# Last batch: weights loaded pairs ahead of their splits, two operands kept raw, last-row transposes first in the queue; v prepared one pair later

## The chip, the cores and the metric

The kernel runs on one core of one Trainium2 chip. The metric is the device time in microseconds; of several runs the median is taken. Smaller is better. The engines are PE (TensorE: matmuls, and PEld for its weight loads), ACT (ScalarE), DVE (VectorE), POOL (GpSimd) and SP (SyncE, which issues nearly all DMAs of this kernel into one queue).

## The reference

Attention without a softmax, gated by `u`, and then a mixture of experts with one expert per token and a capacity.

```python
# u, v: [8, 2496, 256], z: [8, 2496, 64], all float32
scores = (1.0 / S) * np.matmul(z, z.transpose(0, 2, 1))
attn = np.maximum(scores, 0.0) ** 2
x = (u * np.matmul(attn, v)).reshape(B * S, D)          # 19968 x 256

logits = x @ w_gate                                     # 8 experts
expert_idx = np.argmax(logits, axis=1)
gate_w = softmax(logits)[arange(N), expert_idx]
for e in range(8):
    tok_idx = tokens of expert e, the 80 with the largest gate_w
    h = np.maximum(x[tok_idx] @ w1[e], 0.0)             # w1[e]: 256 x 1024
    out[tok_idx] = gate_w[tok_idx, None] * (h @ w2[e])  # w2[e]: 1024 x 256
```

All other rows of the output are zero.

## The kernel before

**Numbers.** A float32 operand of a matmul is split into a high and a low part (`ah` and `al`, two halves of `vt`, `w1h` and `w1l` and so on), and each product takes three matmuls. The high part is a cast on ACT (or DVE), the low part a subtraction on DVE.

**Attention.** Each batch has 20 tiles of 128 tokens. The loop runs over `steps`, which are (batch `b`, chunk `qc` of 512 query tokens, pair `r` of key tiles): 5 chunks of 10 pairs in each of 8 batches. The last chunk has 448 tokens. The scores are symmetric, so a block below the diagonal is not computed a second time: `mirror` transposes it in squares on DVE into a tile `x` and writes that to memory (`y`), and `mirror_back` reads it into a tile `blk` by four DMAs before `mirrored` uses it. A step does this, in this order: the scores of the pair two steps ahead (`scores`: two matmuls a tile into one of three PSUM tiles `s`, the relu on ACT at L316, the square, the cast `ah`, the subtraction `al`, or only the cast at L296 and the subtraction for a mirrored block), the products of its own pair with `v` (`attend`), the bookkeeping of the chunk before (`finished`: the pieces of `x` for the gate, the DMA transposes of `xf` into `xq` by `chunk_store`, the write of `xs` by `chunk_store2`, logits, gate, counts), the loads of the next batch's `z` and `v`, zeros for the output, and in the last batch `weights_ahead`.

**Order.** PE, ACT, DVE and SP issue in the order in which the code is written (`manual_schedule`). Each engine, and the DMA queue of SP, is therefore a line: what waits at its head holds all that stands behind it.

**v of the next batch.** In a batch's last chunk, `prep_v` splits the next batch's five groups of `v`, one at each odd pair: the cast at L105 on ACT, the subtraction at L146 on DVE. Behind the split of group `g` the load of group `g + 2` is issued, since there are two raw buffers, `vraw`.

**Weights ahead.** The 16 weight operands of the 8 experts (`w1` and `w2`) are handled as halves of 512 KB. Ten halves, `order_w`, are loaded and split during the last two chunks of the last batch (`at_w`). A half goes into a raw buffer (`load_raw`; L586) and is split by `split_w` (L596 on ACT, L597 on DVE) in the very next pair. The split parts live in tiles that attention no longer needs (`places`):

```python
for p, raw in list(w_raw.items()):
    split_w(*p, w_raw.pop(p), V)
```

**The end.** After the last pair come the last chunk's `x`, its logits, the gate, the transposes and the write of `xs`, the count, and `blocks`. The expert stage (`ahead`) looks up the tokens of the first two experts, runs `WARM` idle matmuls (4 before the first, 9 before the second lookup's work) on PE, gathers the tokens by an indirect DMA of POOL (`xg<-xs`, L1035), and then runs eight experts, while `split` takes the next half of the weights that are left (their subtraction goes to DVE or POOL) and `loads` issues the load of another.

Of the kernel before, what the change touches and what calls it, by code (L numbers as in the profile page):

```python
# [8 lines left out]
F32 = mybir.dt.float32  # L9
# [10 lines left out]
P = 128  # L20
# [5 lines left out]
def attn_moe_kernel(ctx, tc, zT, uT, v, wg, w1, w2, out, seq, cap):  # L26
# [5 lines left out]
    nc = tc.nc  # L32
    V = nc.vector
    B, _, SP = zT.shape
# [8 lines left out]
    NQ = NT // QT  # L43
# [22 lines left out]
    NA = 4  # L66
# [491 lines left out]
    NPIECE = 2048  # L558
    wt = {}
    n_early = [0]  # L560
    places = []
    late = {}

    def wtile(name):
        if late.get("own"):
            pool, tag = late["own"], "w"
        else:
            i = n_early[0] % (NA + NX + NV + NW)
            n_early[0] += 1
            pool, tag = (places + [(late["pool"], "w")] * NW if "pool" in late else places)[i]  # L570
        return pool.tile([P, NPIECE], F32R, tag=tag, name=f"{name}_{nid()}")

    def load_raw(e, which, part, after=None):

        n = DC if which == 1 else FC
        if which == 1:
            src = w1[e].rearrange("(c p) f -> p c f", p=P)
        else:
            src = w2[e].rearrange("(j p) d -> p j d", p=P)
        pool, tag = (late["raw"], "wraw") if "raw" in late else (zpool, "vraw")  # L580
        raw = pool.tile([P, NPIECE // 2], F32, tag=tag, name=f"wraw_{e}_{which}_{part}")
        rv = raw.rearrange("p (c f) -> p c f", c=n // 2)
        if after:

            after.memset(raw[:, :1], 0.0)
        nc.sync.dma_start(out=rv, in_=src[:, part * n // 2:(part + 1) * n // 2])  # L586
        return rv

    def split_w(e, which, part, rv, eng):
# [19 lines left out]

    ON_V = {(0, 8), (0, 12), (0, 16)}  # L610

    order_w = [(0, 1), (0, 2), (1, 1), (1, 2), (2, 1)]
    at_w = [(NQ - 2, r) for r in (2, 4, 6, 8)] + [(NQ - 1, r) for r in range(1, 7)]
    WAT = {(B - 1,) + at: (*order_w[n // 2], n % 2) for n, at in enumerate(at_w)}
    WARM = 4, 9
    steps = [(b, qc, r) for b in range(B) for qc in range(NQ) for r in range(NP)]
    ET = mybir.EngineType
    v_raw, z_raw, w_raw = {}, {}, {}

    def weights_ahead(b, qc, r):  # L620
        for p, raw in list(w_raw.items()):
            split_w(*p, w_raw.pop(p), V)
        if (b, qc, r) in WAT:
            if not places:

                xt, vv = (sqpool, "x"), (vpool, "vt")
                nb = B * NQ * (NQ - 1) // 2
                a4 = [(apool, f"a{n % NA}") for n in range(nb - NA, nb)]
                places.extend([xt, xt, xt, vv, a4[0], vv, xt, a4[1], a4[2], vv, a4[3], vv, vv, vv])
            p = WAT[b, qc, r]  # L630
            w_raw[p] = load_raw(*p)

    def finished(b, qc, r):

# [41 lines left out]
    with tc.manual_schedule(engines={ET.PE, ET.Activation, ET.DVE, ET.SP}):  # L676
        prep_zc(0, 0, raw0)
        prep_zd(0, 0, raw0)
        prep_zc(0, 1, raw12[:, 0])
        scores(0, 0, 0)  # L680
        prep_v(0, 0, vraw0, nc.scalar, V)
        scores(0, 0, 2)
        v_raw[0, 1] = vraw1
        z_raw.update({(0, 2): raw12[:, 1], (0, 3): raw34[:, 0], (0, 4): raw34[:, 1]})
        constants()
        prev = None
        for i, (b, qc, r) in enumerate(steps):
            last = b == B - 1 and qc == NQ - 1
            now[0] = i
            if r == 0 and prev:  # L690
                chunk_x(*prev)
            if (b, qc) == (0, 0) and r in (0, 2, 4):
                prep_zc(0, r // 2 + 2, z_raw.pop((0, r // 2 + 2)))
            if i + LOOK < len(steps):
                nb, nqc, nr = steps[i + LOOK]
                scores(nb, nqc, 2 * nr)
            if b == 0 and qc == 0:
                if r % 2 == 0 and r < 8:
                    g = r // 2 + 1
# [12 lines left out]
            if r == 2:  # L712
                prep_u(b, qc)
            if b + 1 < B:
                if r == 1:
                    z_raw[b + 1, qc] = load_z(b + 1, qc)
                if r == 9:
                    prep_zc(b + 1, qc, z_raw.pop((b + 1, qc)))
                if qc == NQ - 2 and r == 8:
                    for g in range(2):  # L720
                        v_raw[b + 1, g] = load_v(b + 1, g)
                if qc == NQ - 1:
                    g = r // 2
                    if r % 2 == 1:
                        prep_v(b + 1, g, v_raw.pop((b + 1, g)), nc.scalar, V)
                        if g + 2 < NQ:
                            v_raw[b + 1, g + 2] = load_v(b + 1, g + 2)
            if nb < B and r == 1:
                prep_zd(nb, nqc)
            if r == 5:  # L730
                zero_out(b * NQ + qc, B * NQ)
            if b == B - 1 and qc >= NQ - 2:
                weights_ahead(b, qc, r)
            mirror_back()
            if r == NP - 1:
                prev = b, qc

        chunk_tiles(*prev)
        for kk, c in ((3, 0), (2, 0), (3, 1), (1, 0), (2, 1), (1, 1)):
            attend(*prev, NT - kk, [c])  # L740
            if kk == 1:
                chunk_x_last(*prev, c)
        chunk_logits_last(*prev)
        gate_top(b, NQ - 1, NQ)
        gate(b, NQ - 1, NQ)
        chunk_store(*prev)
        chunk_store2(*prev)
        kb = B * BPB
        count_last(kb - 2, kb)
        blocks(ps_m, "m", gp, oh, kb - 2, kb)  # L750
# [403 lines left out]
    def ahead(empty, block, fetch, pe_table, pe_block, pe_fetch, within, token, whole, ffn_x, ffn_xl,  # L1154
# [2 lines left out]
        ET = mybir.EngineType  # L1157

        pieces = [(e, w, part) for e in range(E) for w in (1, 2) for part in range(2)
                  if (e, w, part) not in WAT.values()]  # L1160
        ready = []

        def loads(n, after=None):
            for p in pieces[:n]:
                ready.append((p, load_raw(*p, after)))
            del pieces[:n]

        def look(i):
            if i < NU:
                block(i)  # L1170
                fetch(i)
                within(i)
# [19 lines left out]
        with tc.manual_schedule(engines={ET.PE, ET.Activation, ET.DVE, ET.Pool}):  # L1192
# [102 lines left out]
```

## Time and profile before

| | |
|---|---|
| median of 3 runs | 1478.59 us (1478.79, 1476.03, 1478.59) |
| the profiled execution | 1480.12 us, span 1478.4 us |
| mean granted TensorE clock | 0.976 |
| PE busy | 1396.2 us (94% of the span) |
| DMA queue of SP | 84.2% of 16 engines' span |
| HBM | 153.48 MB read, 126.46 MB written |

The profiled execution is one more run beside the three. In its page a digit of the second part is the busy share of a fortieth of the span (37 us) in tenths; in a timeline a row has the start, the duration, the engine, the line, the operation with its tiles, and in brackets the idle time before it with what ended it. A row of the waits has an engine and what it was to do, the releaser, the sum, the count and the longest. Names as `blk`, `wraw` and `xs` are the program's.

### The profile page before, as it was taken

The numbers are of one execution on the slowest core, as the hardware profiler recorded it, in microseconds if no ns is written. First come the engines' busy times: TensorE is split into PE (matmuls) and PEld (weight loads), VectorE is DVE, ScalarE is ACT, GpSimd is POOL, SyncE is SP. The second block draws the span as 40 slices with busy tenths as digits, with TensorE's granted clock in tenths as the row PEclk, the third lists the DMA queues.
The fourth block names the chain that finished last, engine by engine and source line by source line (L and its number), as shares of the span: only waits on it lengthen the run. The fifth ranks groups of instructions, "written<-read, shape, count | busy, mean of one in ns | idle before, by whom it ended". The sixth has DMA issues, their size and how long they took to land. (4 is left out here: it accounts for less than half of the span.)

```text
span 1478.4 us, 19494 instructions
## 1 busy us (share of the span) xinstructions
PE 1396.2 (94%) x7083; PEld 1144.3 (77%) x7083; DVE 1078.6 (73%) x1530; ACT 983.7 (67%) x1263; POOL 45.6 (3%) x50
## 2 busy tenths in 40 slices
PE   8999999999999999999999999999999999958587
PEld 6788878887888878887788877887788888846466
DVE  7776788677876788767876688767876688636585
ACT  7776667667776676667776677766776578735264
POOL 0000000000000000000000000000000000000074
PEclk9999999999999999999999999999999999979688
DMA  6799879995999979995999969995999959887363
GB/s 197 209 243 214 211 211 208 238 240 153 253 235 214 235 202 208 237 237 147 232 252 218 253 176 220 238 248 145 229 251 217 260 156 226 225 206 198 70 206 124
DMA packets 300102, 311.97 MB, mean 211 GB/s; under 512 B 136184, under 2 KB 228224, under 8 KB 289760
## 3 DMA queue, kind: packets, MB, share of 16 engines
q1 hardware_dynamic: 299040, 309.11, 84.2%
q0 software_dynamic: 960, 1.56, 0.4%
q8 instruction: 57, 0.93, 0.3%
q14 instruction: 45, 0.37, 0.1%
HBM read 153.48 MB, written 126.46 MB: 189 GB/s over the span
## 5 line engine op out<-in xcount | busy, mean ns | idle before, releaser
L345 PE MATMUL acc<-al,vt 128*128 128x512 f32 (+1 forms) x1520 | 590.6, 389 | 8.0 <-DVE al L54 7.8
L343 PE MATMUL acc<-ah,vt 128*128 128x512 f32 (+1 forms) x1520 | 590.6, 389 | 3.4 <-ACT ah L296 1.6
L344 PE MATMUL acc<-ah,vt 128*128 128x512 f32 (+1 forms) x1520 | 589.1, 388 | 1.2 <-DVE vt L146 1.2
L54 DVE TENSOR_TENSOR al<-a,ah 128x1024 fp32r<-128x1024 f32 (+1 forms) x240 | 291.2, 1213 | 146.8 <-ACT ah L105 137.3
L345 PEld LDWEIGHTS acc<-al,vt 128*128 128x128 f32 x1520 | 287.8, 189 | 67.9 <-DVE al L54 15.3
L343 PEld LDWEIGHTS acc<-ah,vt 128*128 128x128 f32 x1520 | 288.4, 190 | 60.8 <-ACT ah L296 4.6
L344 PEld LDWEIGHTS acc<-ah,vt 128*128 128x128 f32 x1520 | 288.4, 190 | 55.5 <-DVE vt L146 2.0
L316 ACT ACTIVATE a<-s 128x512 f32<-128x512 f32 (+1 forms) x480 | 257.7, 589 | 87.1 <-PE s L313 77.2
L296 ACT CAST ah<-blk 128x1024 fp32r<-128x1024 f32 x160 | 166.3, 1048 | 141.8 <-DMA blk<-y 65.9
L317 ACT ACTIVATE a<-a 128x1024 f32<-128x1024 f32 (+1 forms) x240 | 253.0, 1054 | 7.6
L54 DVE TENSOR_TENSOR al<-blk,ah 128x1024 fp32r<-128x1024 f32 x160 | 192.3, 1214 | 81.7 <-ACT ah L296 80.0
L257 DVE STREAM_TRANSPOSE x<-a 128x512 f32<-128x512 f32 x320 | 207.5, 686 | 0.0
L313 PE MATMUL s<-zd,zc 128*128 128x512 f32 (+1 forms) x480 | 187.4, 391 | 0.1
L105 ACT CAST ah<-a 128x1024 fp32r<-128x1024 f32 x139 | 146.0, 1050 | 4.4
L312 PE MATMUL s<-zc,zc 128*128 128x512 f32 x320 | 131.2, 410 | 5.1 <-ACT a L316 4.9
L107 DVE CAST ah<-a 128x1024 fp32r<-128x1024 f32 (+1 forms) x101 | 68.6, 680 | 49.9 <-ACT a L317 49.7
L313 PEld LDWEIGHTS s<-zd,zc 128*128 128x128 f32 x480 | 90.8, 189 | 15.2 <-issue 0.5
L312 PE MATMUL s<-zc 128*128 128x512 f32 (+1 forms) x160 | 64.9, 406 | 31.0 <-ACT a L316 31.0
L105 ACT CAST vt<-vraw 128x1024 fp32r<-128x1024 f32 (+3 forms) x56 | 45.0, 831 | 65.3 <-DMA vraw<-v 65.3
L146 DVE TENSOR_TENSOR vt<-vraw,vt 128x1024 fp32r<-128x1024 f32 (+1 forms) x40 | 46.7, 1167 | 45.4 <-ACT vt L105 45.2
L312 PEld LDWEIGHTS s<-zc,zc 128*128 128x128 f32 x320 | 60.1, 188 | 23.5 <-ACT a L316 13.4
L373 ACT CAST xb<-xf 128x1024 bf16<-128x1024 f32 (+1 forms) x39 | 40.0, 1027 | 56.7 <-DVE xf L362 56.7
(156 smaller groups left out, 846.6 us busy)
## 6 DMA issues: line engine op xcount, KB each, us to landing
y<-x SPq DMA_DIRECT2D x80, 1024.0 KB, 5.5
blk<-y SPq DMA_DIRECT2D x320, 256.0 KB, 8.2
out<-idle SPq DMA_DIRECT2D x40, 512.0 KB, 5.9
vraw<-v SPq DMA_DIRECT2D x32, 512.0 KB, 8.9
ut<-uT SPq DMA_DIRECT2D x32, 512.0 KB, 5.2
xs<-xq SPq DMA_DIRECT2D x32, 512.0 KB, 7.8
wraw<-w SPq DMA_DIRECT2D x32, 512.0 KB, 5.0
zd<-zc SPq DMA_DIRECT2D x78, 128.0 KB, 3.8
```

What stands on the lines that cost most here:

```text
L54: V.tensor_tensor(out=o, in0=a, in1=b, op=op)
L105: eng.copy(out=o, in_=i)
L107: eng.tensor_copy(out=o, in_=i)
L257: V.transpose(out=x[:, :, :, t].rearrange("p n k s -> p k n s"), in_=a)
L296: nc.scalar.copy(out=natural(ah), in_=src)
L312: nc.tensor.matmul(s[:, :nq], zk, zc[:, :nq], start=True, stop=False)
L313: nc.tensor.matmul(s[:, :nq], zk, zd[:, :nq], start=False, stop=True)
L316: nc.scalar.activation(out=a[:, h, :nq], in_=s[:, :nq], func=AF.Relu)
L317: nc.scalar.activation(out=a[:, :, :nq], in_=a[:, :, :nq], func=AF.Square)
L343: nc.tensor.matmul(o, vt[:, t, 0, cs], ah, start=k == 0, stop=False)
L344: nc.tensor.matmul(o, vt[:, t, 1, cs], ah, start=False, stop=False)
L345: nc.tensor.matmul(o, vt[:, t, 0, cs], al, start=False, stop=False)
```

## The change

1. In the last batch, the loads and splits of weights have two tables, `LOADS` and `SPLITS`. Eight halves (experts 0 and 1) are loaded at pairs 6 and 7 of chunk 2, 0, 2, 5 and 8 of chunk 3, and 2 and 4 of chunk 4; they are split at pairs 0, 2, 5 and 8 of chunk 3 and 2, 4, 5 and 7 of chunk 4. A half's load stands behind the split of the half two before it, in whose raw buffer it lands.
2. Both halves of expert 2's `w1` (at pair 4 of chunk 4) and of its `w2` (pair 6) are loaded into free tiles of attention and stay unsplit (`kept`). The expert stage splits them: one more `split(V, V)` ahead of the first expert's tokens, and the others where the next halves were split before. The list `places` is written anew for that, and `loads` counts the buffers that the kept ones do not use.
3. `WARM` is 4 and 12.
4. `chunk_store` of the last chunk is written ahead of its logits and gate.
5. `prep_v` stands at pairs 2, 4, 6, 8 and 9 of the last chunk.

```diff
+    early = [(e, w, part) for e in range(2) for w in (1, 2) for part in range(2)]
+    qa, qb, qz = NQ - 3, NQ - 2, NQ - 1
+    LOADS = dict(zip([(qa, 6), (qa, 7), (qb, 0), (qb, 2), (qb, 5), (qb, 8), (qz, 2), (qz, 4)], early))
+    SPLITS = dict(zip([(qb, 0), (qb, 2), (qb, 5), (qb, 8), (qz, 2), (qz, 4), (qz, 5), (qz, 7)], early))
+    RAW = {(qz, 4): (2, 1), (qz, 6): (2, 2)}
-    order_w = [(0, 1), (0, 2), (1, 1), (1, 2), (2, 1)]
-    at_w = [(NQ - 2, r) for r in (2, 4, 6, 8)] + [(NQ - 1, r) for r in range(1, 7)]
-    WARM = 4, 9
+    WARM = 4, 12
...
-    def weights_ahead(b, qc, r):
-        for p, raw in list(w_raw.items()):
-            split_w(*p, w_raw.pop(p), V)
+    def weights_ahead(qc, r):
...
+        if (qc, r) in SPLITS:
+            p = SPLITS[qc, r]
             split_w(*p, w_raw.pop(p), V)
+        if (qc, r) in LOADS:
+            p = LOADS[qc, r]
             w_raw[p] = load_raw(*p)
+        if (qc, r) in RAW:
+            e, which = RAW[qc, r]
+            pool, tag = late["kept"].pop(0)
+            raw = pool.tile([P, NPIECE], F32, tag=tag, name=f"wall_{e}_{which}")
+            for part in range(2):
+                rv, src = raw_part(raw[:, part * NPIECE // 2:(part + 1) * NPIECE // 2], e, which, part)
+                nc.sync.dma_start(out=rv, in_=src)
+                kept.append(((e, which, part), rv))
...
                 if qc == NQ - 1:
-                    g = r // 2
-                    if r % 2 == 1:
+                    g = (r - 1) // 2 if r < 9 else 4
+                    if r in (2, 4, 6, 8, 9):
                         prep_v(b + 1, g, v_raw.pop((b + 1, g)), nc.scalar, V)
...
+        chunk_store(*prev)
         chunk_logits_last(*prev)
         gate_top(b, NQ - 1, NQ)
         gate(b, NQ - 1, NQ)
-        chunk_store(*prev)
         chunk_store2(*prev)
...
-        ready = []
+        ready = list(kept)
         def loads(n, after=None):
+            n = min(n, NR - sum(1 for r in ready if r not in kept))
...
             look(3)
+            split(V, V)
             whole(0)
```

The next two pieces are the SP queue in the last batch, from the middle of chunk 2 to the middle of chunk 3, before and after. A row is a line, the DMA, and its tiles: `wraw_1_0` is the raw half 0 of a `w1`, `y_4_2` a block of scores written for chunk 4, `blk_3_2` one that is read for chunk 3; the number at the end of a name only counts.

```order
L236 DMA out<-idle 128x4x256
L261 DMA y_4_2_11909<-x_4_2_11852 128x2048
L278 DMA blk_3_2_11923<-y_3_2_11823 32x4x512 x4
L278 DMA blk_4_0_11928<-y_4_0_11263 32x4x512 x4
L278 DMA blk_4_1_11963<-y_4_1_11625 32x4x512 x4
L412 DMA_TRANSPOSE xq_2_12009<-xf_2_11968 128x8x128 x2
L120 DMA zd_4_12012<-zc_4_10974 64x512
L121 DMA zd_4_12012<-zc_4_10974 64x512
L278 DMA blk_4_2_12015<-y_4_2_11909 32x4x512 x4
L159 DMA ut_3_12037<-uT 128x2x512
L586 DMA wraw_1_0_12039<-w 128x1024
```

```order
L236 DMA out<-idle 128x4x256
L589 DMA wraw_1_0_11893<-w 128x1024
L261 DMA y_4_2_11911<-x_4_2_11852 128x2048
L589 DMA wraw_1_1_11925<-w 128x1024
L278 DMA blk_3_2_11927<-y_3_2_11823 32x4x512 x4
L278 DMA blk_4_0_11932<-y_4_0_11263 32x4x512 x4
L278 DMA blk_4_1_11967<-y_4_1_11625 32x4x512 x4
L589 DMA wraw_2_0_12000<-w 128x4x256
L412 DMA_TRANSPOSE xq_2_12019<-xf_2_11972 128x8x128 x2
L120 DMA zd_4_12022<-zc_4_10974 64x512
L121 DMA zd_4_12022<-zc_4_10974 64x512
```

The first half stood behind the blocks, the transposes and `ut`; now two halves stand ahead of `blk_3_2`, and the third ahead of the transposes.

ACT in the same place, at the start of chunk 3, before and after: `w1h` is the cast of a weight half, `ah_3_8` that of a mirrored block, `a_3_12` the relu of a computed one.

```order
L373 CAST xb_2_11969<-xf_2_11968 128x1024
L296 CAST ah_3_6_11992<-blk_3_1_11655 128x1024
L296 CAST ah_3_8_12020<-blk_3_2_11923 128x1024
L381 CAST xb_2_11969<-xr_2_11970 128x1024
L296 CAST ah_3_10_12041<-blk_3_2_11923 128x1024
L596 CAST w1h_52_12059<-wraw_1_0_12039 128x1024
L316 ACTIVATE a_3_12_12063<-s_3_12_12064 128x512
```

```order
L373 CAST xb_2_11973<-xf_2_11972 128x1024
L599 CAST w1h_52_11996<-wraw_1_0_11893 128x1024
L296 CAST ah_3_6_12002<-blk_3_1_11655 128x1024
L296 CAST ah_3_8_12030<-blk_3_2_11927 128x1024
L381 CAST xb_2_11973<-xr_2_11974 128x1024
L599 CAST w1h_52_11996<-wraw_1_1_11925 128x1024
L296 CAST ah_3_10_12053<-blk_3_2_11927 128x1024
L316 ACTIVATE a_3_12_12071<-s_3_12_12072 128x512
```

The first cast of a weight moved three places up, and the second one is now among the mirrored blocks of this chunk too.

The end of the SP queue, from the loads of the last chunk to the first expert's, before and after; `wall` is an operand that is kept raw, `xs<-gall` the write of the gate, `wtab` that of the lookup table, `xs<-xq` the last row's `x`.

```order
L586 DMA wraw_1_1_12465<-w 128x1024
L555 DMA wtab<-wb_12520 64x256
L586 DMA wraw_2_0_12654<-w 128x4x256
L586 DMA wraw_2_1_12656<-w 128x4x256
L501 DMA xs<-gall 128x4x1 x2
L412 DMA_TRANSPOSE xq_4_12580<-xf_4_12523 128x7x128 x2
L1255 TENSOR_LOAD flag
L1255 ISA x2
L421 DMA xs<-xq_4_12580 128x6x256
```

```order
L647 DMA wall_2_12460<-w 128x4x256 x2
L555 DMA wtab<-wb_12516 64x256
L589 DMA wraw_1_0_12650<-w 128x1024
L412 DMA_TRANSPOSE xq_4_12542<-xf_4_12519 128x7x128 x2
L589 DMA wraw_1_1_12652<-w 128x1024
L501 DMA xs<-gall 128x4x1 x2
L421 DMA xs<-xq_4_12542 128x6x256
```

The transposes moved ahead of the gate's write and of one half of the experts' own loads.

ACT in the last chunk of batch 6, where the groups of the next batch's `v` are cast (`vt_0` to `vt_2`), before and after:

```order
L296 CAST ah_4_6_10731<-blk_4_1_10431 128x1024
L105 CAST vt_0_10753<-vraw_0_10681 128x4x256
L296 CAST ah_4_8_10761<-blk_4_2_10485 128x1024
L381 CAST xb_3_10708<-xr_3_10709 128x1024
L296 CAST ah_4_10_10780<-blk_4_2_10485 128x1024
L105 CAST vt_1_10798<-vraw_1_10683 128x4x256
L296 CAST ah_4_12_10803<-blk_4_3_10702 128x1024
```

```order
L296 CAST ah_4_6_10731<-blk_4_1_10431 128x1024
L296 CAST ah_4_8_10756<-blk_4_2_10485 128x1024
L381 CAST xb_3_10708<-xr_3_10709 128x1024
L105 CAST vt_0_10775<-vraw_0_10681 128x4x256
L296 CAST ah_4_10_10780<-blk_4_2_10485 128x1024
L296 CAST ah_4_12_10798<-blk_4_3_10702 128x1024
L105 CAST vt_1_10814<-vraw_1_10683 128x4x256
```

Each cast of `v` is one mirrored block later.

More of the change, by code (lines that the diff above doesn't have):

```diff
@@ L560, in attn_moe_kernel @@
     n_early = [0]
-    places = []
+    places, kept = [], []
     late = {}
@@ L567, in wtile, with raw_part @@
         else:
-            i = n_early[0] % (NA + NX + NV + NW)
+            i = n_early[0] % len(places)
             n_early[0] += 1
-            pool, tag = (places + [(late["pool"], "w")] * NW if "pool" in late else places)[i]
+            pool, tag = places[i] or (late["pool"], "w")
         return pool.tile([P, NPIECE], F32R, tag=tag, name=f"{name}_{nid()}")
-    def load_raw(e, which, part, after=None):
+    def raw_part(raw, e, which, part):
         n = DC if which == 1 else FC
@@ L579, in load_raw @@
             src = w2[e].rearrange("(j p) d -> p j d", p=P)
+        return raw.rearrange("p (c f) -> p c f", c=n // 2), src[:, part * n // 2:(part + 1) * n // 2]
+    def load_raw(e, which, part, after=None):
         pool, tag = (late["raw"], "wraw") if "raw" in late else (zpool, "vraw")
         raw = pool.tile([P, NPIECE // 2], F32, tag=tag, name=f"wraw_{e}_{which}_{part}")
-        rv = raw.rearrange("p (c f) -> p c f", c=n // 2)
         if after:
             after.memset(raw[:, :1], 0.0)
-        nc.sync.dma_start(out=rv, in_=src[:, part * n // 2:(part + 1) * n // 2])
+        rv, src = raw_part(raw, e, which, part)
+        nc.sync.dma_start(out=rv, in_=src)
         return rv
@@ L610, in attn_moe_kernel @@
     ON_V = {(0, 8), (0, 12), (0, 16)}
-    order_w = [(0, 1), (0, 2), (1, 1), (1, 2), (2, 1)]
-    at_w = [(NQ - 2, r) for r in (2, 4, 6, 8)] + [(NQ - 1, r) for r in range(1, 7)]
-    WAT = {(B - 1,) + at: (*order_w[n // 2], n % 2) for n, at in enumerate(at_w)}
-    WARM = 4, 9
+    early = [(e, w, part) for e in range(2) for w in (1, 2) for part in range(2)]
[4 more added lines that the diff above has]
+    WARM = 4, 12
     steps = [(b, qc, r) for b in range(B) for qc in range(NQ) for r in range(NP)]
@@ L618, in attn_moe_kernel @@
     v_raw, z_raw, w_raw = {}, {}, {}
-    def weights_ahead(b, qc, r):
-        for p, raw in list(w_raw.items()):
-            split_w(*p, w_raw.pop(p), V)
[L623 to L630, printed above, removed]
-            w_raw[p] = load_raw(*p)
+    def weights_ahead(qc, r):
+        if not places:
+            xt, vv = (sqpool, "x"), (vpool, "vt")
+            nb = B * NQ * (NQ - 1) // 2
+            a4 = [(apool, f"a{n % NA}") for n in range(nb - NA, nb)]
+            late["kept"] = [xt, a4[2]]
+            places.extend([xt, xt, xt, vv, a4[0], vv, a4[1], vv, a4[3], vv, vv])
+            places.extend([None] * NW + [vv, xt, a4[2]])
+        if (qc, r) in SPLITS:
+            p = SPLITS[qc, r]
+            split_w(*p, w_raw.pop(p), V)
+        if (qc, r) in LOADS:
+            p = LOADS[qc, r]
+            w_raw[p] = load_raw(*p)
+        if (qc, r) in RAW:
[4 more added lines that the diff above has]
+                rv, src = raw_part(raw[:, part * NPIECE // 2:(part + 1) * NPIECE // 2], e, which, part)
+                nc.sync.dma_start(out=rv, in_=src)
+                kept.append(((e, which, part), rv))
     def finished(b, qc, r):
@@ L731, in attn_moe_kernel @@
                 zero_out(b * NQ + qc, B * NQ)
-            if b == B - 1 and qc >= NQ - 2:
-                weights_ahead(b, qc, r)
+            if b == B - 1 and qc >= NQ - 3:
+                weights_ahead(qc, r)
             mirror_back()
@@ L1159, in ahead @@
         pieces = [(e, w, part) for e in range(E) for w in (1, 2) for part in range(2)
-                  if (e, w, part) not in WAT.values()]
-        ready = []
+                  if (e, w, part) not in early and (e, w) not in RAW.values()]
+        ready = list(kept)
         def loads(n, after=None):
+            n = min(n, NR - sum(1 for r in ready if r not in kept))
             for p in pieces[:n]:
```

## The prediction

> **What bounds the kernel now.** I read the page's two first parts, then the waits, the SP queue and the windows of the last 120 us. The slices of the page are 37 us each.
>
> ```profile
> PE 1396.2 (94%) x7083; PEld 1144.3 (77%) x7083; DVE 1078.6 (73%) x1530; ACT 983.7 (67%) x1263; POOL 45.6 (3%) x50
> PE   8999999999999999999999999999999999958587
> PEclk9999999999999999999999999999999999979688
> DMA  6799879995999979995999969995999959887363
> ```
>
> TensorE (PE) bounds all but the end: its digit is 9 up to slice 35. Only slices 36 to 40 fall to 5, 8, 5, 8 and 7, with the granted clock at 6 to 9 tenths. They hold the last two chunks of the last batch, the last row and the experts. What ends PE's and ScalarE's (ACT's) idle time there, between 1270 and 1410 us (sum, count, longest):
>
> ```profile
> PE s L312 <- ACT a L316: 19.8, 2, 15.9
> PE wp L550 <- ACT tot L513: 9.2, 1, 9.2
> ACT w1h L596 <- DMA wraw<-w: 30.3, 3, 18.3
> ACT w2h L596 <- DMA wraw<-w: 9.2, 2, 5.4
> ```
>
> PE waits for scores that ACT has not read out of PSUM, and ACT stands at the cast of a weight half whose load has not landed: ACT does in order what is written, so one late load holds the relu behind it and the next score. The timeline shows the two ends of the worst case and the later one on the same pattern:
>
> ```profile
> 1319.06 1.04 ACT L596 CAST w1h<-wraw 128x1024 fp32r<-128x1024 f32 x1 [18.33 <-DMA wraw<-w]
> 1320.65 0.80 PE L312 MATMUL s<-zc 128*128 128x512 f32 x1 [15.93 <-ACT a L316]
> 1383.02 1.04 ACT L596 CAST w1h<-wraw 128x1024 fp32r<-128x1024 f32 x1 [10.85 <-DMA wraw<-w]
> 1384.23 0.27 PE L550 MATMUL wp<-upper,oh 128*64 128x128 bf16 x1 [9.24 <-ACT tot L513]
> ```
>
> Why the load is late stands in the SP queue. It is one line of transfers in order, and the load of 1310.74 was issued behind the blocks and the two transposes:
>
> ```profile
> 1287.80 10.13 SPq L278 DMA_DIRECT2D blk<-y  x12
> 1298.87 8.01 SPq L412 DMA_TRANSPOSE xq<-xf  x2
> 1310.74 0.47 SPq L586 DMA_DIRECT2D wraw<-w  x1
> 1389.44 0.94 SPq L586 DMA_DIRECT2D wraw<-w  x2
> 1394.88 2.58 SPq L412 DMA_TRANSPOSE xq<-xf  x2
> 1399.74 0.54 SPq L426 DMA_DIRECT2D xs<-xq  x1
> 1404.85 1.09 POOL L1035 DMA_INDIRECT xg<-xs,tok  x1 [1402.30 <-issue]
> ```
>
> And the queue itself: windows between 1288.5 us and the first gather of tokens at 1404.85. After the stretch come its length, the busy time of PE, PEld, DVE, ACT and POOL with their counts, the granted clock, the DMA engines' mean busy share, and GB/s.
>
> ```profile
> 1288.50:1326.00 37.50, 21.57 (x85) 17.31 (x84) 14.17 (x14) 12.15 (x14) 0.00 (x0) 0.77 1.02 241
> 1326.00:1338.50 12.50, 12.50 (x78) 10.24 (x77) 7.83 (x11) 9.34 (x11) 0.00 (x0) 1.00 0.06 22
> 1338.50:1369.00 30.50, 23.49 (x122) 19.87 (x121) 19.92 (x23) 14.56 (x17) 0.00 (x0) 0.91 0.87 231
> 1369.00:1374.50 5.50, 5.50 (x18) 4.94 (x17) 4.78 (x12) 3.14 (x5) 0.00 (x0) 0.57 0.08 1
> 1374.50:1383.50 9.00, 0.49 (x5) 0.26 (x4) 1.16 (x2) 0.48 (x1) 0.00 (x0) 0.65 0.63 60
> 1383.50:1391.00 7.50, 6.77 (x36) 5.98 (x35) 4.08 (x14) 1.04 (x3) 0.00 (x0) 0.74 0.07 9
> 1391.00:1404.00 13.00, 7.52 (x35) 3.72 (x35) 9.50 (x71) 1.32 (x4) 0.00 (x0) 0.74 0.58 151
> ```
>
> The pattern is a lockstep. While the queue is full (1.02), PE has 21.6 of 37.5 us; when the load has landed PE runs and the queue is empty (0.06), since nothing was written ahead. Neither resource is full over the stretch. Share times length, added up over the seven rows, gives 38.3 + 0.8 + 26.5 + 0.4 + 5.7 + 0.5 + 7.5 = 79.7 us of full queue. The gather comes 116.35 us after 1288.5, so 36.7 us are left in which the queue has room.
>
> **The last batch.** The loads are moved three to seven pairs ahead of their splits and spread over three chunks, so a cast on ACT no longer waits for a load issued one pair before. What is late next is the queue as a whole: the blocks, transposes and weights of this stretch are needed before the gather whatever their order. The halves that this stretch loads, and the window just ahead of it:
>
> ```profile
> wraw<-w SPq DMA_DIRECT2D x12, 512.0 KB, 5.1
> 1286.00:1288.50 2.50, 2.50 (x13) 2.07 (x12) 2.50 (x5) 1.05 (x1) 0.00 (x0) 1.00 0.12 52
> ```
>
> One half piece is 0.524 MB, and at the 241 GB/s of the first row it takes 2.2 us. The stretch of before held 12 halves. Of the new kernel the first goes out ahead of 1288.5, in a gap that the queue had there (0.12); behind it up to the gather I count 13 (seven early halves, the four of the two raw operands, and two of the experts' own). That is one more.
>
> Queue work to the gather: 79.7 + 2.2 = 81.9 us. Of the 36.7 us with room, 2.2 are used up by that piece, and I leave some 4 us of holes: the last transposes, the write of x that waits for their landing, and the gather behind it cannot overlap (by the rows at 1394.88, 1399.74 and 1404.85, issue to issue, about 5 us a step; part of that runs under work). So 36.7 - 2.2 - 4 = 30.5, which I take as **-31 us**. Bounds: with 10 us of holes -25, with none and one half pushed behind the gather -37; below that nothing speaks, because the queue was full with the very same transfers.
>
> Does PE then bind instead? Its busy time times the granted clock, over the first six windows, is 16.6 + 12.5 + 21.4 + 3.1 + 0.3 + 5.0 = 58.9 us at full clock; attention, which ends near 1389.4 now, would end at 1347 with no hole in it and near 1350 with small ones, earlier than the queue's 1370 (1288.5 + 81.9). PE is ready first; I price its recovery at nothing beyond the 31.
>
> **The last row's transposes ahead of the logits.** They are written in front of the gate's two small writes and so leave the queue earlier by those, but the two raw operands (four halves, 8.8 us) now stand ahead of them. Since the queue has a backlog then, their place in it changes the sum by nothing; if PE bound, the transposes and the write of x would be what follows the end of attention, and the 5.4 us between the rows of 1389.44 and 1394.88 could go. 0, between -5 and 0.
>
> **The two operands kept raw.** The two splits of expert 2's w1 leave the attention and go in front of the first expert. The rows are DVE's wait for the first gather, its subtraction for a weight half (count, busy, mean ns, idle before), and the window of the experts:
>
> ```profile
> 1407.71 0.45 DVE L1048 COPY xf<-xg 80x512 uint16<-80x512 uint16 x1 [5.42 <-DMA xg<-xs,tok]
> L597 DVE TENSOR_TENSOR w1l<-wraw,w1h 128x1024 fp32r<-128x1024 f32 x14 | 21.3, 1528 | 27.9 <-ACT w1h L596 27.9
> 1404.85:1478.40 73.55, 57.14 (x368) 45.70 (x368) 49.28 (x99) 40.71 (x70) 43.67 (x32) 0.87 0.50 166
> ```
>
> Two casts on ACT at 1.04 and two subtractions on VectorE (DVE) at 1.53, the second cast beside the first subtraction, take 1.0 + 3.1 = 4.1 us. That fits into DVE's idle 5.42, so 0; without the cover +4. The rest of the experts reads one half less from the queue behind the gather, but the queue is at 0.50 there and does not hold it: 0, between -3 and +3.
>
> **Three more warm matmuls** (12 for 9) run on an idle PE ahead of the first gather:
>
> ```profile
> L171 PE MATMUL warm<-idle 128*128 128x512 bf16 x22 | 8.6, 562 | 1.4 <-POOL idle L166 1.4
> 1408.22 0.53 PE L1057 MATMUL xp<-ident,xf 80*128 80x80 f32 x2 [5.92 <-DVE xf L1048]
> 1408.20:1414.40 6.20, 5.80 (x16) 3.61 (x17) 4.16 (x19) 2.01 (x4) 3.96 (x8) 0.50 0.34 79
> ```
>
> PE's first expert row waits 5.92 us and the 6.2 us from there run at half clock. The 22 warm matmuls are 8.6 us of busy time, so three add some 1.2 (a mean of 562 ns counts their overlap), and the wait shrinks to about 4.7. I take 0, between -3 (6.2 us at full clock instead of half) and +1.2. The Trainium skill, page "TensorE: Matmul & The Clock Gate", section "Part 1: The HAM clock gate", says that about 3.4 us of a busy PE warm it, and what is issued before that runs at half rate. By that rule PE would have to be kept busy for 3.4 us up to the gather's landing, and three matmuls more do not reach into the wait; the trace agrees with the half rate (0.50 over 6.2 us), and at most 3.1 us could be won.
>
> **v one pair later.** In the last chunk of each of seven batches ACT waits for the next batch's v (150 to 1290 us):
>
> ```profile
> ACT vt L105 <- DMA vraw<-v: 61.2, 21, 4.4
> PE s L312 <- ACT a L316: 14.4, 23, 2.2
> PE acc L345 <- DVE al L54: 5.3, 10, 0.8
> 1174.34 1.04 ACT L105 CAST vt<-vraw 128x1024 fp32r<-128x1024 f32 x1 [4.03 <-DMA vraw<-v]
> 1175.88 0.74 PE L312 MATMUL s<-zc 128*128 128x448 f32 x1 [1.70 <-ACT a L316]
> ```
>
> Of ACT's 61.2 us only 14.4 + 5.3 = 19.7 reach PE, 2.8 a batch. The casts now stand a pair later (3.4 us: 38 chunks of ten pairs end near 1289 us), but each load is issued behind its predecessor's split, so the third load falls behind the two zd copies and ut, 0.79 MB or 3.3 us at 241 GB/s. For that piece the later cast and the later landing cancel, and its 1.70 us remains; for the first, whose load does not move, the wait goes. 2.8 - 1.7 = 1.1 a batch, times seven: **-7 us**. Bounds: -14 (most of the 19.7 goes) and +5 (the third and fourth pieces land later than a pair).
>
> Sum against the profiled execution: 1480.1 - 31 - 7 = 1442.1. The median of the runs lies 1.5 below it (1478.59 and 1480.12), so 1440.6, **1441 us**.
>
> **The rivals.** A is this forecast: the queue binds to the gather, 1441, its own range 1431 to 1452 (the ends of two terms do not fall together).
>
> What the queue moved between 1286 and 1404 us:
>
> ```profile
> DMA packets 23350, 19.07 MB, mean 162 GB/s; under 512 B 12000, under 2 KB 19376, under 8 KB 23088
> ```
>
> B: the queue is faster when it never runs dry, and PE binds. Attention ends near 1350, 39 us earlier, and the transposes in front give 4 more: 1480.1 - 43 - 7 - 1.5, about 1428. Against it: the engines are already full at 241 GB/s (1.02), and half of the packets are under 512 B. The Trainium skill, page "DMA: Bandwidth & Descriptors", section "Specifications", gives about 358 GB/s of HBM for a core. By that figure the 19.6 MB of this stretch would take an estimated 55 us instead of 81.9, and the queue could not bind; the trace does not agree, with 241 GB/s where the engines show no room.
>
> C: the splits still stand in ACT's order ahead of relus, and their loads behind blocks, transposes and the writes of x. If three of the halves (those split at pairs 5 and 8 of chunk 3 and at pair 5 of chunk 4) each still come about 4 us late, some 13 us of the 29.0 stay; the clock of 0.77 behind such waits costs 5 more (21.6 us busy times 0.23), and what is issued behind them slips by some 8. Attention then ends near 1376, the gather follows as now 15.4 us later, at 1391 instead of 1405: 1480.1 - 14 - 7 - 1.5, about 1458. For it: the new kernel puts each load behind the split of two before, so one late split delays the next load.
>
> D, the other side: ACT's wait for v reaches PE whole. Moving the casts nearer to the score's relu could expose up to 61.2 - 19.7 = 41.5 us; from 51 of the 61.2 upwards (19.7 + 31) the kernel is slower; all of it gives 1480.1 - 31 + 41.5 - 1.5, about 1489. Against it: three PSUM score buffers have hidden two thirds so far.
>
> E: the loads, issued earlier, delay the blocks as much as they gain, and the time stays at 1478.6.
>
> **How the numbers follow.** A .64, B .13, C .18, D .03, E .02. The range 1426 to 1459 takes in B and C and the bounds of A's terms (-37 and -14 give 1428, -25 and +5 give 1459). Anything beyond 0.2% (3 us), about what a measurement tells from no change here, counts: A, B and C are faster (.95), E the same, D slower.
>
> **What would show it.** Right: a DMA share of 0.95 or more from 1280 to about 1363 without a hole of over 5 us; ACT's waits at w1h and w2h from 30.3 and 9.2 to under 10 together; the first gather at about 1367 (1404.85 - 31 - 7); 73.5 us, give or take 3, from it to the end; ACT's v waits under 25 and PE's score waits of 150 to 1290 from 14.4 to about 7. Wrong: a queue with holes and PE at 9 to the end (B); the same 10 us waits of PE in the last two chunks (C); a rise of PE's score waits before 1290 (D).

## The result and the profile after

The changed kernel takes 1438.61 us, the median of four runs (1435.10 to 1442.42), beside 1478.69 for the four runs of the kernel before that were made with it. The ratio is 0.9729, 95% interval 0.9694 to 0.9764. Run twice more, as the yardstick for other kernels, it gave 0.9762 (0.9738 to 0.9785) and 0.9712 (0.9696 to 0.9728), so 35 to 43 us. Forecast were 1441 us and a range of 1426 to 1459. Its profiled execution took 1441.15 us, span 1439.4.

The first two parts of the page after:

```profile
PE 1385.3 (96%) x7086; PEld 1135.8 (79%) x7086; DVE 1074.9 (75%) x1530; ACT 983.1 (68%) x1263; POOL 47.5 (3%) x48
PE   8999999999999999999999999999999999999687
PEclk9999999999999999999999999999999999999899
DMA  6799978996999959997899959999598979999944
```

PE's digit is 9 now up to slice 37; the 5 and 8 of the last two chunks are gone, and so are the dips of the clock there. The waits of 1270 to 1410 us, which answer to the four rows at the start of the prediction (the range reaches into the experts here):

```profile
PE s L312 <- ACT a L316: 2.0, 1, 2.0
ACT w2h L599 <- DMA wraw<-w: 10.4, 4, 4.5
ACT w1h L599 <- DMA wraw<-w: 3.7, 3, 2.0
```

The same view from 1278 to 1347 us alone, the end of the attention:

```profile
PE wp L550 <- ACT tot L513: 0.3, 1, 0.3
PE acc L343 <- ACT ah L296: 2.0, 2, 1.5
ACT w2h L599 <- DMA wraw<-w: 9.8, 3, 4.5
ACT ah L296 <- DMA blk<-y: 7.2, 2, 5.4
```

PE's 29.0 us in these two waits became 2.3. Up to the end of the attention ACT still waits 9.8 us for weights, where it was 39.5 (30.3 + 9.2), in pieces of at most 4.5 us, and at most 2.0 of that reaches a score; the other 4.3 of the 14.1 above are in the expert stage. New in this view is the last row, 7.2 us at the casts of mirrored blocks. The longest wait, 5.4 us, ends 9.7 us after chunk 2's `x` (1289.90), for a block that is now issued behind two weight halves; in the kernel before the wait at the same cast (4.4 us, put down to PE there) ends 8.3 us after it (1297.79).

Four events mark the stages in both traces: the end of batch 6 (its `x` on DVE), the `x` of the last batch's chunk 2, the last matmul of the attention, and the first gather. Before:

```profile
1191.11 1.15 DVE L362 SCALAR_TENSOR_TENSOR xf<-acc,ut 128x448 f32<-128x448 f32 x2
1289.53 1.28 DVE L362 SCALAR_TENSOR_TENSOR xf<-acc,ut 128x512 f32<-128x512 f32 x2
1389.05 0.37 PE L348 MATMUL acc<-al,vt 128*128 128x448 f32 x1
```

After, with the first gather:

```profile
1181.87 1.16 DVE L362 SCALAR_TENSOR_TENSOR xf<-acc,ut 128x448 f32<-128x448 f32 x2
1280.22 1.28 DVE L362 SCALAR_TENSOR_TENSOR xf<-acc,ut 128x512 f32<-128x512 f32 x2
1346.74 0.37 PE L348 MATMUL acc<-al,vt 128*128 128x448 f32 x1
1366.63 1.09 POOL L1052 DMA_INDIRECT xg<-xs,tok  x1 [1364.08 <-DMA wraw<-w]
```

By these, 9.2 us were won ahead of the end of batch 6 (1191.11 to 1181.87), where only the place of `v` differs. From chunk 2's `x` to the end of attention it was 99.9 us and is 66.9: 33.0 won. From there to the gather it was 15.4 and is 19.5: 4.1 lost. From the gather to the end it was 73.55 and is 72.77: 0.8 won. With 0.1 between batch 6 and chunk 2 this is the 39.0 us by which the spans differ.

What the 33.0 us are made of shows in a window over that stretch, before and after (length, busy times of PE, PEld, DVE, ACT and POOL, clock, DMA share, GB/s); it starts 1.03 us ahead of chunk 2's `x`, where the sums of the prediction start:

```profile
1288.50:1389.42 100.92, 68.73 (x322) 57.01 (x320) 51.25 (x71) 40.71 (x49) 0.00 (x0) 0.81 0.71 168
1279.19:1347.11 67.92, 61.70 (x320) 50.13 (x318) 47.72 (x66) 38.45 (x47) 0.00 (x0) 1.00 1.02 241
```

PE was idle for 32.2 us of it and is for 6.2: 26.0 us. The other 7.0 us are matmuls, as many as before within 1% (322 and 320 in the traces), that were busy for 68.7 us at a granted clock of 0.81 and are for 61.7 at 1.00. So a fifth of the gain is the clock.

The same stages of every run, from its own trace (us; the end of batch 6, then three lengths):

| kernel | end of batch 6 | chunk 2's x to end of attention | to the first gather | to the end | ratio of times to before, 95% |
|---|---|---|---|---|---|
| before | 1191.1 | 99.9 | 15.4 | 73.6 | 1 |
| changed | 1181.9 | 66.9 | 19.5 | 72.8 | 0.9729 (0.9694-0.9764) |
| changed, `again` | 1185.6 | 66.0 | 20.4 | 72.6 | 0.9762 (0.9738-0.9785) |
| changed, `yard` | 1183.9 | 66.3 | 21.2 | 73.4 | 0.9712 (0.9696-0.9728) |
| `v_only` | 1183.7 | 101.4 | 15.4 | 72.6 | 0.9949 (0.9931-0.9967) |
| `near` | 1182.2 | 97.5 | 13.6 | 73.3 | 0.9905 (0.9890-0.9921) |
| `less_dma` | 1177.6 | 66.8 | 19.6 | 74.3 | 0.9729 (0.9715-0.9742) |
| `more_dma` | 1180.5 | 70.6 | 23.9 | 72.7 | 0.9767 (0.9749-0.9785) |
| `store_old` | 1185.6 | 65.9 | 22.2 | 75.1 | 0.9764 (0.9747-0.9781) |
| `warm9` | 1185.1 | 66.2 | 20.1 | 73.6 | 0.9745 (0.9730-0.9760) |
| `no_raw` | 1177.6 | 65.6 | 16.8 | 74.2 | 0.9725 (0.9708-0.9743) |
| `late` | 1184.9 | 67.8 | 12.4 | 76.8 | 0.9700 (0.9683-0.9716) |
| `hole` | 1187.4 | 68.8 | 16.1 | 72.8 | 0.9742 (0.9723-0.9761) |
| `best` | 1186.8 | 68.6 | 11.9 | 78.8 | 0.9710 (0.9696-0.9723) |

The stages of the last batch repeat within a microsecond or two between the three traces of the changed kernel; the end of batch 6 does not. The ratios were measured in three sessions: `again`, `v_only`, `store_old` and `warm9` together; `less_dma`, `more_dma`, `near` and `late`; `yard`, `hole`, `best` and `no_raw`. The second session has no run of the changed kernel, so its ratios stand beside yardsticks of the other two, and its kernels are read from their stages. Each row of stages is one trace.

### The profile page after: what moved, and what is told of

Read it like the earlier page. It is cut to its first block, busy times and chain, and to the rows that moved or that the text cites. A ratio compares the mean times of both kernels' runs of the same rounds, so it can differ in the third digit from the quotient of the medians.

```text
span 1439.4 us, 19509 instructions
## 1 busy us (share of the span) xinstructions
PE 1385.3 (96%) x7086; PEld 1135.8 (79%) x7086; DVE 1074.9 (75%) x1530; ACT 983.1 (68%) x1263; POOL 47.5 (3%) x48
## 3 DMA queue, kind: packets, MB, share of 16 engines
q1 hardware_dynamic: 299040, 309.11, 86.3%
## 5 line engine op out<-in xcount | busy, mean ns | idle before, releaser
L345 PEld LDWEIGHTS acc<-al,vt 128*128 128x128 f32 x1520 | 285.7, 188 | 66.8 <-DVE al L54 14.4
L316 ACT ACTIVATE a<-s 128x512 f32<-128x512 f32 (+1 forms) x480 | 257.6, 588 | 83.1 <-PE s L313 73.4
L107 DVE CAST ah<-a 128x1024 fp32r<-128x1024 f32 (+1 forms) x101 | 68.6, 679 | 46.6 <-ACT a L317 46.6
L313 PEld LDWEIGHTS s<-zd,zc 128*128 128x128 f32 x480 | 90.4, 188 | 15.4 <-issue 0.5
L146 DVE TENSOR_TENSOR vt<-vraw,vt 128x1024 fp32r<-128x1024 f32 (+1 forms) x40 | 46.7, 1167 | 27.8 <-ACT vt L105 27.6
```

The lines of the kernel that those rows point to most:

```text
L107: eng.tensor_copy(out=o, in_=i)
L313: nc.tensor.matmul(s[:, :nq], zk, zd[:, :nq], start=False, stop=True)
L316: nc.scalar.activation(out=a[:, h, :nq], in_=s[:, :nq], func=AF.Relu)
L345: nc.tensor.matmul(o, vt[:, t, 0, cs], al, start=False, stop=False)
```

## The experiments

**The changed kernel as yardstick.**

> The changed kernel itself, as the yardstick for the variants that run beside it. From its four runs (1435.1 to 1442.4): 1436 to 1442 us, 36 to 42 us under the kernel before.

> The changed kernel again, as the yardstick on the chip of these runs: 36 to 42 us under the kernel before.

36 and 42 us under the kernel before (1446.09 beside 1482.05 us, 1441.61 beside 1483.28), as expected; the first time itself lies above the 1436 to 1442 us, but the kernel before was slower in that session too.

**v alone.** The kernel before, with

```diff
-                    g = r // 2
-                    if r % 2 == 1:
+                    g = (r - 1) // 2 if r < 9 else 4
+                    if r in (2, 4, 6, 8, 9):
```

> The kernel before with v prepared one pair later and nothing else. Theory (the third load's 1.7 us of PE wait remains in each batch, the rest of the 2.8 us goes): 7 us faster, by the ends of batch 6 in the two traces (1191.11 and 1181.87) up to 9.2 us: 1469 to 1472 us, ACT's v waits of 150 to 1290 us at about 26 us as in the changed kernel, PE's score waits at about 7. The tail from the end of batch 6 to the gather stays as before, 213.7 us. Rival (most of the 19.7 us goes): 14 us faster, 1464. Other rival (the gain comes only with the weights' change): 1478.

1474.53 us beside 1482.05: 0.9949, so 7.5 us faster (4.9 to 10.2), as forecast; neither rival lies in the interval. Its tail to the gather is that of before (101.4 + 15.4 us). ACT's waits of 150 to 1290 us in it are 27.6 us. PE's waits for scores are 9.6 us, not the 7 expected, so of the 7.5 us 4.8 can be read in them. In the changed kernel they are:

```profile
ACT vt L105 <- DMA vraw<-v: 26.2, 8, 5.0
PE s L312 <- ACT a L316: 7.2, 12, 1.8
PE acc L345 <- DVE al L54: 5.3, 11, 0.6
```

Twenty-one waits for `v` became eight. The score waits halved from 14.4, and those for `al` stayed at 5.3. The third group in batch 6 is the one that remains, with its score behind it:

```profile
1169.23 1.05 ACT L105 CAST vt<-vraw 128x1024 fp32r<-128x1024 f32 x1 [3.47 <-DMA vraw<-v]
1170.77 0.50 PE L312 MATMUL s<-zc 128*128 128x512 f32 x1 [0.72 <-ACT a L316]
```

Its wait on ACT is 3.47 us where it was 4.03, so the later cast and the later landing nearly cancel, as the prediction had it; PE's part is 0.72 us, not the 1.70 that I had left in place.

**The distance between load and split.** The changed kernel with the loads moved to one pair ahead of each split:

```diff
-    LOADS = dict(zip([(qa, 6), (qa, 7), (qb, 0), (qb, 2), (qb, 5), (qb, 8), (qz, 2), (qz, 4)], early))
+    LOADS = dict(zip([(qa, 9), (qb, 1), (qb, 4), (qb, 7), (qz, 1), (qz, 3), (qz, 4), (qz, 6)], early))
```

> The changed kernel with each of the eight early halves loaded one pair before its split, as the kernel before did; the splits, their spread over chunks 3 and 4, and all else stay. Theory (the distance between load and split is what frees PE): ACT's waits at w1h and w2h rise from 14 to over 30 us again, PE's score waits in the tail return to 10 us or more, and 10 to 20 us of the 29 us gained in the tail are lost: 1449 to 1459. Rival (the wider spread of the splits, and two halves fewer in the attention, is what helps): within 3 us of the changed kernel.

1466.76 us: 0.9905, where the changed kernel had 0.971 to 0.976. Attention's last stretch is back at 97.5 us of 99.9: 30.6 us are lost, more than the 10 to 20 that I expected. Waits of PE and ACT from 1270 us on:

```profile
PE acc L343 <- ACT ah L296: 13.8, 2, 8.8
PE wp L550 <- ACT tot L513: 13.0, 1, 13.0
ACT w2h L599 <- DMA wraw<-w: 25.0, 3, 13.0
ACT w1h L599 <- DMA wraw<-w: 19.3, 4, 12.7
```

ACT waits 44.3 us for weights, and PE behind it 26.8: at the cast of mirrored blocks, and at the count of the first four chunks, where it stood 9.2 us before. The waits for scores, which I expected back at 10 us or more, are 1.8 us: the late weights reach PE by another way. So 30.6 of the 33.0 us hang on the distance; the fewer splits and their spread over the chunks bring 2.4 us without it, hardly more than the stage scatters. Whether the distance would bring as much with the splits where they were was not run.

**Is the queue what sets the gather?** My forecast rested on this. The DMA share of the changed kernel does look like it (window, length, busy times, clock, share, GB/s):

```profile
1278.06:1366.63 88.57, 72.34 (x377) 56.72 (x375) 62.20 (x145) 42.66 (x54) 0.00 (x0) 0.94 1.01 233
1340.00:1350.00 10.00, 8.37 (x50) 6.86 (x48) 8.16 (x26) 2.63 (x5) 0.00 (x0) 1.00 0.78 140
1350.00:1366.60 16.60, 7.53 (x36) 3.80 (x36) 11.69 (x73) 3.21 (x6) 0.00 (x0) 0.69 1.07 230
```

It is full over the whole stretch, but with a dip at the end of attention. I took work out of it, and put work in (two kernels, marked at the ends of the lines):

```diff
-            if r == 5:
+            if r == 5 and (b, qc) not in ((B - 1, NQ - 2), (B - 1, NQ - 1)):     # less_dma
                 zero_out(b * NQ + qc, B * NQ)
...
                 zero_out(b * NQ + qc, B * NQ)
+                if (b, qc) in ((B - 1, NQ - 2), (B - 1, NQ - 1)):                # more_dma
+                    zero_out(b * NQ + qc, B * NQ)
```

> The changed kernel without the zeros written to the output at pair 5 of the last batch's chunks 3 and 4 (two writes of 512 KB; these rows of the output are left out). Theory (the queue is full to the gather, 241 GB/s): 4.4 us less queue work, 4 us faster than the changed kernel, 2 us where PE's end of attention at 1347 does not move. Rival (PE's attention and the chain behind it set the gather): 0 to 1 us.

> The changed kernel with these two writes of zeros issued twice. Theory (the queue is full to the gather): 4.4 us slower than the changed kernel, gather near 1371. Rival (PE sets it): 0 to 1 us slower.

Two writes less, 4.4 us of the queue by my price, moved nothing: chunk 2's `x` to the gather takes 86.3 us (1275.95 to 1362.30), beside 86.4. Over the attention's part of it the DMA share fell from 1.01 to 0.94, and that part took 66.8 us beside 66.9. The window of `less_dma` that answers to 1340 to 1350 above (its events come 4.3 us earlier) shows where the time went:

```profile
1336.00:1346.00 10.00, 8.00 (x48) 6.49 (x46) 8.16 (x28) 2.30 (x5) 0.00 (x0) 1.00 0.47 35
```

The dip deepened from 0.78 to 0.47, 3.1 us of the 4.4. It is made by SP's order and not by a lack of work. SP of the changed kernel:

```profile
1334.61 0.46 SPq L236 DMA_DIRECT2D out<-idle  x1
1342.90 1.35 SPq L501 DMA_DIRECT2D xs<-gall  x2
1344.30 1.71 SPq L647 DMA_DIRECT2D wall<-w  x2
1348.82 6.50 SPq L412 DMA_TRANSPOSE xq<-xf  x2
1358.91 0.53 SPq L426 DMA_DIRECT2D xs<-xq  x1
```

After the zeros at 1334.6 SP stands for 7.8 us at the write of the gate, which DVE has not computed, and the raw `w2`, which needs nothing, stands behind it. What lies ahead of that point runs into the dip and is free; what lies behind it stands ahead of the last row's transposes. More writes did cost 8.1 us (86.4 to 94.5), twice their work, but that run is no clean test of traffic: SP spends 10.26 us on the two writes of the last chunk (0.46 on the one in the changed kernel), because the second write of the same rows waits for the first, and that holds the gate's write and all behind it. The wait stands in the view of SP's waits from 1330 us on:

```profile
SPq L236 <- DMA out<-idle: 9.4, 1, 9.4
```

**The transposes.** Back behind the gate:

```diff
-        chunk_store(*prev)
         chunk_logits_last(*prev)
         gate_top(b, NQ - 1, NQ)
         gate(b, NQ - 1, NQ)
+        chunk_store(*prev)
```

> The changed kernel with the last row's transposes behind its logits and gate again. Theory (the queue has a backlog there, so their place is worth nothing, or the 1 to 2 us by which the gate's end at about 1357 us exceeds the backlog): 0 to 2 us slower than the changed kernel, its gather at 1367 to 1369. Rival (their place sets the gather, so the whole 8 us between their issue at 1348.8 and the gate's write at 1356.2 comes back): 8 us slower, about 1447.

End of attention to gather 22.2 us, beside 19.5, 20.4 and 21.2: 1 to 3 us, near the 0 to 2 of the first theory and far from the 8 of the rival. In the times nothing can be seen (0.9764 and 0.9762).

**The warm matmuls.** `WARM = 4, 9`.

> The changed kernel with 9 warm matmuls instead of 12 before the first gather. Theory (three short matmuls do not reach into the 6.5 us of waiting for the gather): within 1 us of the changed kernel, clock 0.5 to 0.6 in the first 6.2 us of the first expert. Rival (they keep the clock): up to 3 us slower.

0.9745 beside 0.9762, intervals overlapping; 73.6 us in the experts beside 72.6. The clock of the 6.2 us from its first expert matmul (1372.92) is 0.68, above the 0.5 to 0.6 expected and beside 0.62 in the changed kernel, with waits of PE of 7.9 and 6.5 us ahead of it. The three matmuls do nothing that can be measured.

**The raw operands.** `RAW = {}`, so their halves are loaded by the expert stage.

> The changed kernel without the two operands kept raw: their four halves are loaded in the expert stage like the others. Theory (they fill the hole at the end of attention only in part, and the stage waits for its first halves without them): the gather 4 us earlier, since two of these halves stood ahead of the transposes, the expert stage 4 to 8 us longer, 0 to 4 us slower than the changed kernel. Rival (they only stand in the way): 4 us faster.

The gather comes 4 to 5 us earlier (65.6 + 16.8 = 82.4 us, beside 86.4 to 87.5) and the experts take 74.2 us, 1 us or so longer. The times are the same: 0.9725 beside 0.9712. Both halves of the first theory are there, the second smaller than the 4 to 8 us that I put it at.

**What stands ahead of the transposes.** Two kernels issue less ahead of them. `late` loads the raw `w2` behind the last row's write of `x`, and the stage's own first halves behind the first gathers:

```diff
-    RAW = {(qz, 4): (2, 1), (qz, 6): (2, 2)}
+    RAW = {(qz, 4): (2, 1)}
...
         blocks(ps_m, "m", gp, oh, kb - 2, kb)
+        load_whole(2, 2)
...
-            loads(2)
...
                 token(i)
+            loads(2, PL)
             look(2)
             look(3)
-            split(V, V)
+            split(V, V, after=PL)
```

> The changed kernel with the raw w2 of expert 2 and the expert stage's own first four halves issued behind the last row's write of x (the latter behind the first two gathers), so that transposes and x stand first in the queue at the end of attention. Theory (from the trace of the changed kernel: attention ends at 1347.1 but the gather comes 19.5 us later, against 15.4 before, because the transposes took 7.4 us and x 6.9 us to land behind these halves): the gather about 5 to 6 us earlier, at 1360 to 1362; the experts lose 0 to 3 us, since their loads start later; 2 to 6 us faster than the changed kernel. Rival (the experts need these halves at once, and what is saved at the gather is given back): 0, or up to 3 us slower.

`hole` only moves the raw `w2` one pair up, ahead of the gate's write: `RAW = {(qz, 4): (2, 1), (qz, 5): (2, 2)}`.

> The changed kernel with the raw w2 of expert 2 loaded at pair 5 of chunk 4 instead of pair 6, so ahead of the gate's write, for which SP waited 7.8 us while the queue ran down to a share of 0.53. Theory (what is issued ahead of that write lies in the hole and is free; what is issued behind it stands ahead of the last row's transposes and sets the gather): two halves, 4.4 us, leave the way, attention's end to gather falls from 19.5 to 15 or 16 us, 4 us faster than the changed kernel. Rival (the queue is full to the gather as a whole, so the place of two halves in it is worth nothing): 0.

The price of the place is confirmed in both: end of attention to gather 12.4 us in `late`, 16.1 in `hole`, for 19.5 to 21.2. But neither keeps it whole. In `hole` the attention itself takes 68.8 us for 66 to 67, and the ratio, 0.9742 beside 0.9712, shows no gain. Those 2 us are the clock: PE is busy there for 63.0 us at a granted clock of 0.95, where `yard` has 60.8 at 1.00 (`late` and `best` have 0.95 as well, `again` 0.97). Whether the edit brings that about is not shown. In `late` the experts take 76.8 us for 73. Rows of `late`, DVE and PE, on the way to the second and third expert:

```profile
1372.36 0.47 DVE L1050 TENSOR_SCALAR_CACHE_REDUCE lw<-wr,rin 80x256 bf16<-80x256 bf16 x1 [4.25 <-DMA wr<-wtab,idx]
1373.36 0.92 POOL L1055 DMA_INDIRECT xg<-xs,tok  x1 [4.35 <-DVE tok L60]
1375.25 0.46 PE L1101 MATMUL hp<-w1h,xTl 128*80 128x512 f32 x1 [4.31 <-DVE xTl L54]
```

The lookup `wr` of the third expert lands 9 us after the first gather (`lw` in the changed kernel: 6.7 us after it), and both the third gather and, in DVE's order, the second expert's low part stand behind it. The third gather comes 9.9 us after the first, where the changed kernel has 7.7:

```profile
1374.36 0.91 POOL L1052 DMA_INDIRECT xg<-xs,tok  x1 [2.83 <-DVE tok L60]
```

The lookup `wr` of `late` was issued at 1366.24, right behind the first of the halves that the edit had moved there (1366.07), and `lw` starts 6.1 us later; in the changed kernel it is 4.1 us (1369.24 to 1373.36).

**Both together,** with the second expert's low part ahead of that lookup on DVE, and the loads behind the lookups:

```diff
-    RAW = {(qz, 4): (2, 1), (qz, 6): (2, 2)}
+    RAW = {(qz, 4): (2, 1), (qz, 5): (2, 2)}
...
-            loads(2)
...
             look(2)
             look(3)
-            split(V, V)
+            loads(2, PL)
+            split(V, V, after=PL)
...
                     spread(1)
+                    ffn_x(1)
+                    ffn_xl(1)
                     take(2)
...
-                elif i + 1 < NU:
+                elif i and i + 1 < NU:
```

> As the run before, and the expert stage's own first four halves issued behind the first two gathers and the two lookups, and the second expert's transposed tokens split ahead of the third's lookup on DVE (in the earlier run with late loads PE waited 4.3 us there behind a lookup that landed late). Theory: attention's end to gather 12.5 us as in that run, the expert stage back from 76.8 to 73 us or a little over, 5 to 7 us faster than the changed kernel. Rival (the experts need the halves at once): the stage stays at 76 to 77 us, 2 to 3 us faster.

It has the shortest way to the gather, 11.9 us, and the longest expert stage, 78.8. The ratio is 0.9710 beside 0.9712: nothing. My reason for the stage's length in `late` was therefore not enough; I removed that wait of PE, and the stage grew by 2 us. The third gather still comes 9.2 us after the first, and now it lands late itself. DVE's copy of the third expert's tokens, in `best` and in the changed kernel:

```profile
1380.61 0.45 DVE L1065 COPY xf<-xg 80x512 uint16<-80x512 uint16 x1 [3.03 <-DMA xg<-xs,tok]
1377.25 0.45 DVE L1065 COPY xf<-xg 80x512 uint16<-80x512 uint16 x1
```

It starts 5.8 us after the gather (1374.84), beside 2.9 (1374.36): in `best` the four moved halves were issued at 1371.76, just ahead of it. From the first gather to the fifth it takes 22.8 us in `best`, 20.7 in `late` and 18.5 in the changed kernel; from the fifth to the end 56.0, 56.1 and 54.3. So most of what `best` loses, and half of what `late` does, is lost at these first small transfers, with the moved halves in their way. The rival's reason, experts that need the halves at once, does not show: ACT waits for weights in this stage 5.1 us in `best`, 4.9 in `late` and 7.6 in the changed kernel. That the halves are the whole cause is not shown. No kernel tried is shown to beat the changed one; `late`, at 0.9700, ran in another session than its yardsticks.

## Why the prediction was right, and where it was not

The total was right: 39.0 us between the profiled executions against 38 forecast. So were the gather (1367 forecast, 1366.6 measured), the stage behind it (73.5 and 72.8) and PE's score waits up to 1290 us (7 and 7.2). ACT's waits for `v` were to be under 25 us and are 26.2; those for weights under 10 together and are 9.8 up to the end of the attention, 14.1 in the whole window. The DMA share, which was to be 0.95 or more without a hole of over 5 us, is 1.01 in all, but has the dip to 0.78 from 1340 to 1350.

- **v, -7 us.** Right in size (-7.5 by `v_only`). The profile's 9.2 lies inside the scatter of that part of the program. What it was made of was not right: I counted the 5.3 us of waits for `al` as `v`'s, and they are still 5.3, while of the 11.9 us of score waits that I let stand (1.70 a batch) 7.2 are left (9.6 in `v_only`). The two errors cancel, which is luck.
- **The last batch, -31 us.** It measures -28.9, but the step behind it failed. I wrote that the queue sets the gather, that "PE is ready first" and that its recovery is priced at nothing. `less_dma` shows that queue work inside the attention is not what sets the gather, and the stages show that it is PE's recovery that counts: 33.0 us, and then a loss of 4.1. My estimate of PE's work to the end of attention, 58.9 us, measures 61.7 at a clock of 1.00, in a stretch of 67.9. The order of what SP issues counts in the 19.5 us behind it (12.4 in `late`, 16.1 in `hole`). My term was a sum over the whole queue that came near by the balance of the two; that was luck.
- **The count of halves** failed too: I had 13 ahead of the gather. Fifteen are issued in the window 1278.06 to 1366.63, since two more of the experts' own follow the last row's write at 1360.3 (DMA issues: count, KB each, us to landing):

```profile
wraw<-w SPq DMA_DIRECT2D x11, 512.0 KB, 7.2
wall<-w SPq DMA_DIRECT2D x4, 512.0 KB, 9.7
```

  Share times length is 89.5 us, not 81.9, and there are no 4 us of holes in sum: the dip at the end of attention (0.78 over 10 us) is made up by shares above 1 elsewhere. Behind the gather my own count left two halves fewer than before (18 for 20), not the one that I wrote there.
- **B, PE bound** (1428) was the right mechanism for the attention, where it gave 39 us and 33.0 were won. The transposes were to give 4 us more, but do not leave at once, and the way to the gather grew by as much. **C** was there in small: halves of `w2` do wait (9.8 us on ACT up to 1347), and PE has 2.0 us of waits for a score. So was **E**: the block at the start of chunk 3 is cast 1.4 us later, counted from chunk 2's `x` (9.7 for 8.3).
- **The transposes** at 0, but for a wrong reason: with the backlog that the raw operands make, their place is worth 1 to 3 us (`store_old`). That the gather follows them once the backlog is gone (`late`, 12.4 us) is likely but not shown, as no view gives the landing of `x` there.
- **Raw operands and warm matmuls** at 0: in the times `no_raw` and `warm9` agree.
- **The two rules of the Trainium skill.** On the clock ("TensorE: Matmul & The Clock Gate", "Part 1: The HAM clock gate") the traces agree: with 6.5 us of waiting ahead of the first expert the clock of the 10 us from the gather is 0.66 in the changed kernel. In `late` PE waits only 2.1 us and has 1.00; in `best` it waits 2.8 and has 0.83:

```profile
1366.63:1376.63 10.00, 6.03 (x19) 3.57 (x20) 4.26 (x20) 2.97 (x6) 5.91 (x7) 0.66 0.19 44
1363.41:1373.41 10.00, 5.04 (x23) 2.51 (x21) 4.91 (x16) 3.44 (x6) 4.88 (x9) 1.00 0.79 256
1365.64:1375.64 10.00, 6.84 (x25) 3.88 (x24) 6.30 (x27) 2.58 (x6) 6.08 (x9) 0.83 0.39 118
```

The rows are of the changed kernel, `late` and `best`, each from its first gather on. The same section of the Trainium skill gives one idle window of about 3.4 us as what brings the half rate. The wait of `best`, 2.8 us, is below that, and yet its clock fell; in `late`, where the clock was kept, the stage gained nothing by it. On the queue ("DMA: Bandwidth & Descriptors", "Specifications", 358 GB/s) the rate that fills the engines depends on what is moved. `no_raw`, with almost nothing but weights in the queue:

```profile
1368.33:1378.33 10.00, 8.25 (x61) 6.49 (x60) 9.06 (x27) 7.59 (x14) 5.96 (x5) 1.00 0.99 335
```

335 GB/s at a share of 0.99, near the figure of the Trainium skill and far above the 241 at 1.02 that I took for everything. A half costs 1.6 us at that rate, not 2.2.

## What to carry to other kernels

On in-order engines and an in-order queue, a load must be issued so far ahead that all that stands before it in the queue has landed when its consumer is reached; here the distance was worth 30.6 us of attention (`near`). A full queue does not prove that the queue binds: take a known piece of work out of it and see whether the end moves, and look for the wait at the head of the issuing engine that makes its dips. Before the last dependent chain of a stage, ask what stands ahead of it in the queue that could have gone earlier or later, and follow the gain to the next consumer before counting it: what is moved out of the way of one small transfer can stand in the way of the next.

## What was not expected

- Up to the end of batch 6 the changed kernel and its variants (`v_only` aside) issue the same program, and yet that point lies between 1177.6 and 1187.4 us in their traces, while the stages behind it repeat to a microsecond or two. Effects below some 5 us are lost in the times and could be read only from the stages.
- The expert stage does not start its clock at the first gather: brought forward by 4 to 7 us in `late`, `no_raw` and `best` (counted from chunk 2's `x`), the gather is followed by a stage that is 1 to 6 us longer.
